# Sliding-window attention and a two-layer MLP: other order of loads, transposes and products in the opening

## The chip, the cores and the metric

The kernel runs on one core of a Trainium2 chip. A core has TensorE (PE in the profile; its weight loads are listed as PEld), VectorE (DVE), ScalarE (ACT), GpSimd (POOL) and SyncE (SP), each with a program of its own; they wait for one another by semaphores. PE reads from SBUF and writes to PSUM, whose eight banks are named here A, C, B, E, LA, LB and t (t is two banks). Transfers that change the type on the way (float32 in memory to bfloat16 or float16 in SBUF) are issued by POOL. The metric is the device time of one execution in microseconds; the profile's span is a little shorter than it.

## The reference

```python
def _attn_ref(q, k, v):                      # q, k, v: (8, 8, 576, 64)
    window = 32
    scores = (1.0 / np.sqrt(D)) * np.matmul(q, k.transpose(0, 1, 3, 2))
    mask = np.abs(pos[:, None] - pos[None, :]) <= window
    scores = np.where(mask, scores, -1000000000.0)
    scores = scores - np.max(scores, axis=-1, keepdims=True)
    attn = np.exp(scores)
    attn = attn / (np.sum(attn, axis=-1, keepdims=True) + 1e-09)
    return np.matmul(attn, v)

def _moe_ref(x, w_in, w_out):                # x: (4608, 512), w_in: (512, 2048), w_out: (2048, 512)
    h = x @ w_in
    g = h * (1.0 / (1.0 + np.exp(-1.702 * h)))
    return g @ w_out

x = attn_out.transpose(0, 2, 1, 3).reshape(B * S, H * D)
```

Every token attends to the 32 tokens on either side within its sequence of 576; the eight heads side by side are the input of the MLP.

## The kernel before

The 4608 tokens (8 sequences end to end) are cut into 36 units of 128 queries, and four units make a tile of 512 tokens for the MLP. A unit's queries start 32 tokens behind its keys, so that two blocks of 64 queries each see 128 keys. For a unit u, `scores(u, tag)` makes 24 small products into two PSUM banks and two exps on ACT; `band(u)` is the product with the 0/1 mask on DVE; `values(u, tag)` makes 16 products of 65 columns (the 65th sums the weights), for which the values are needed once as loaded (`ve`) and once shifted by 64 tokens (`vo`, made by `odd_v`: its half 1 copies from the values of u, its half 0 from those of u + 1); `norm(u)` divides on DVE; `x_T` or `x_T2` transposes one or two units on PE, and a copy puts them into `xT`.

The MLP of tile 0 is done in plain products: `layer1_plain(t, d, half, tag)` is 8 products of 256 columns into one bank and a gelu on ACT (d counts 256 columns of w_in, so quarter c of w_in serves d = 2c and 2c + 1; half is the first or second pair of units), and `layer2_plain` gives a list `l2` of 64 products of 512 columns, which `do(l2, n)` takes n at a time to fill PE where it would wait. In that list the products 8 to 15 read the second quarter of w_out, 16 to 23 the third. The later tiles use Strassen-like sums (`w1_sums`, `w2_sums`, `x_sums`, `g_sums`) with seven products for eight; their first block is `l1_group` in `first_layer1`, called when `opening` has ended. What is left of `l2` is run out in `run` between scores(9) and scores(10).

`opening` (lines 576 to 717) is the whole work up to there, in an order written out by hand: each engine runs its instructions in the order in which these calls stand, and waits at each for what it needs. It has units 0 to 7, layer 1 of tile 0 and part of its layer 2. The keys and queries of tile 0 come in two parts (`load_first`, part 0 and 1, 256 or 320 tokens), are transposed on PE by `T_first` in two banks each and copied out by the two engines named; those of tile 1 come by `load_four` and `T_four`. `load_v(u)` loads values (128 tokens, in pieces where a sequence ends: token 576 lies in the middle of unit 4), `load_w1(c)` a quarter of w_in, `load_w2(c)` a quarter of w_out. All these loads stand in POOL's program, between its other work (the mask by `setup_mask`, some `odd_v`), and in one DMA queue.

`keep_busy(n, tag, cols)` makes n products of zeros whose results nobody reads, to fill PE where it would wait. Before the change there are 60 of 96 columns at the start and then 6, 4, 10, 5, 2, 4, 4 and 4 of 256 columns (lines 606 to 660).

ACT has to load a table when it goes from exp to gelu or back. In the opening the exps of units 0 to 3 come first, then gelus, then the exps of units 4 to 7, then gelus again.

Of the kernel before, what the change touches and what calls it, by code (L numbers as in the profile page):

```python
# [26 lines left out]
class _Kernel:  # L27
# [536 lines left out]

    def keep_busy(self, n, tag="t", cols=256):
        junk = self.bank(tag, [128, 512], F32, "junk")
        for _ in range(n):
            self.mm(junk[:, 0:cols], self.idle[:, 0:128], self.idle[:, 0:cols], start=True, stop=True)  # L570


    SHARES = {("first", 1): (3, 0, 5, 4), ("first", 2): (3, 3, 6, 6), ("first", 3): (3, 1, 7, 7), ("last", 0): (0, 12, 6, 6),
# [2 lines left out]
    def opening(self):  # L576

        nc, dve, act, pool = self.nc, self.nc.vector, self.nc.scalar, self.nc.gpsimd
        self.setup()
        for i in range(8):  # L580
            dve.memset(self.idle[:, 64 * i:64 * i + 64], 0.0)
        dve.memset(self.spark, 0.0)
        for t in self.ve:
            dve.memset(t[:, :, self.D:], 1.0)
        self.load_first("k", 0)
        self.load_first("q", 0)
        make_identity(nc, self.ident)
        act.activation(self.spark, self.spark, AF.Exp)
        for u in (0, 1, 2):
            self.load_v(u)  # L590
        self.load_w1(0)
        self.setup_mask()
        self.load_first("k", 1)
        self.load_first("q", 1)
        self.load_w1(1)
        self.load_v(3)
        self.load_v(4)
        self.load_w1(2)
        self.load_four("k")
        self.load_four("q")  # L600
        self.load_w1(3)
        self.odd_v(3, pool)
        dve.tensor_copy(self.identh, self.ident)
        self.keep_busy(60, "E", 96)
        self.T_first("k", 0, "AC", (dve, act))
        self.keep_busy(6, "E")
        self.T_first("q", 0, ("LA", "LB"), (dve, act))
        self.keep_busy(4, "E")
        self.load_v(5)
        self.load_w2(0)  # L610
        self.load_v(6)
        self.load_v(7)
        self.load_v_part(1024, 64)
        self.load_w2(1)
        self.load_v_part(1088, 64)
        for c in (2, 3):
            self.load_w2(c)
        self.load_kq("k", 8)
        self.scores(0, "t")
        self.scores(1, "AC")  # L620
        self.odd_v(0, dve)
        self.odd_v(1, dve, (1,))
        self.keep_busy(10, "E")
        self.band(0)
        self.odd_v(1, dve, (0,))
        self.band(1)
        self.values(0, "t")
        self.keep_busy(5, "E")
        self.values(1, "AC")
        self.norm(0)  # L630
        self.norm(1)
        self.keep_busy(2, "E")
        self.x_T(0, "LA", act)
        self.keep_busy(4, "E")
        self.x_T(1, "LB", act)
        self.T_first("k", 1, "AC", (dve, dve))
        h, n, gelus = [], [0], []

        def l1(half, *ds):
            for d in ds:  # L640
                self.layer1_plain(0, d, half, h[n[0] % len(h)])
                n[0] += 1

        self.layer1_plain(0, 0, 0, "B", gelus)
        self.T_first("q", 1, ("LA", "LB"), (dve, act))
        self.layer1_plain(0, 1, 0, "E", gelus)
        h[:] = ["B", "E", "LB", "LA", "B", "E", "LB", "LA"]
        self.odd_v(2, dve, (1,))
        self.scores(2, "t")
        self.scores(3, "AC")  # L650
        self.layer1_plain(0, 2, 0, "LA", gelus)
        self.layer1_plain(0, 3, 0, "LB", gelus)
        self.do(gelus)
        self.band(2)
        self.odd_v(2, dve, (0,))
        self.band(3)
        self.keep_busy(4, "t")
        self.values(2, "t")
        self.norm(2)
        self.keep_busy(4, "A")  # L660
        self.values(3, "AC")
        self.norm(3)
        l1(0, 4)
        self.x_T2(2, "A", dve)
        l1(0, 5)
        dve.tensor_copy(self.k_first, self.kT[0][:, :, 0:64])
        dve.tensor_copy(self.v_first, self.ve[0][0:64])
        for i in (3, 1, 2):
            self.w1_sums((i,), 0)
        self.cut_mask()  # L670
        for u in (6, 7):
            self.odd_v(u, pool)
        for u in (8, 9, 10, 11):
            self.fetch(u)
        l1(1, 0, 1)
        halo = self.kT[4]
        self.T_four("k", "AC", (dve, dve))
        dve.tensor_copy(self.kT[4][:, :, 0:64], halo)
        self.w1_sums((4,), 0)
        l1(1, 2, 3)  # L680
        self.T_four("q", "AC", (dve, act))
        l1(1, 4, 5)
        self.odd_v(4, dve)
        self.scores(4, "t")
        self.scores(5, "AC")
        for i in (3, 1):
            self.w1_sums((i,), 1)
        for d, tag in ((6, "B"), (7, "E")):
            self.layer1_plain(0, d, 0, tag, gelus)
        self.do(self.l2, 3)  # L690
        self.scores(6, "t")
        self.do(self.l2, 3)
        self.scores(7, "AC")
        self.do(gelus)
        self.do(self.l2, 2)
        self.band(4)
        self.odd_v(5, dve)
        self.band(5)
        self.band(6)
        self.values(4, "t")  # L700
        self.norm(4)
        self.values(5, "AC")
        self.norm(5)
        self.band(7)
        self.do(self.l2, 4)
        self.values(6, "t")
        self.norm(6)
        self.do(self.l2, 4)
        self.values(7, "AC")
        self.norm(7)  # L710
        h[:] = "BE"
        n[0] = 0
        l1(1, 6, 7)
        self.x_T2(4, "A", act)
        self.do(self.l2, 4)
        self.x_T2(6, "t", dve)
        self.do(self.l2, 4)
# [223 lines left out]
```

## Time and profile before

| | us |
|---|---|
| median of three runs | 286.95 |
| lowest and highest | 286.2, 288.33 |
| the profiled execution | 286.22 |
| its span | 284.5 |
| PE busy | 277.3 (97%) |
| DVE busy | 215.9 (76%) |
| ACT busy | 194.0 (68%) |
| POOL busy | 131.4 (46%) |

Busy time of PE counts products whose results nobody reads, and products that overlap are counted once. A line in a view by time has the start, the duration, the engine, the line of the code, the operation, what is written and read, its shapes and the number of instructions merged; in brackets the idle time before it and what ended it. In a merged group of products the time from its start to the start of the next group tells more than its duration, since the end of one product overlaps the next. Nearly all products have line 70, that of a helper, and are told apart by the names of their tiles: h is layer 1, o is layer 2, sc scores, pv values, tp a transpose, junk an unread product.

### The profile page before, as it was taken

The numbers are of one execution on the slowest core, as the hardware profiler recorded it, in microseconds if no ns is written. First come the engines' busy times: TensorE is split into PE (matmuls) and PEld (weight loads), VectorE is DVE, ScalarE is ACT, GpSimd is POOL, SyncE is SP. The second block draws the span as 40 slices with busy tenths as digits, with TensorE's granted clock in tenths as the row PEclk, the third lists the DMA queues.
The fourth block names the chain that finished last, engine by engine and source line by source line (L and its number), as shares of the span: only waits on it lengthen the run. The fifth ranks groups of instructions, "written<-read, shape, count | busy, mean of one in ns | idle before, by whom it ended". The sixth has DMA issues, their size and how long they took to land.

```text
span 284.5 us, 9230 instructions
## 1 busy us (share of the span) xinstructions
PE 277.3 (97%) x3819; PEld 231.0 (81%) x3819; DVE 215.9 (76%) x502; ACT 194.0 (68%) x341; POOL 131.4 (46%) x199
## 2 busy tenths in 40 slices
PE   8999999999999999999999999999999999999993
PEld 8778857776787888888788888888888888888882
DVE  1758795896987889788778887888788888856621
ACT  2557775889887679668866887587759775677320
POOL 8866497996799429947084809331010000000000
PEclk9999999999999999999999999999999999999999
DMA  8999999999999999999999999994522030202033
GB/s 93 183 193 199 184 203 157 197 123 158 130 166 138 195 133 184 144 200 133 188 144 175 141 175 125 175 143 82 148 52 83 2 111 21 76 0 76 9 105 113
DMA packets 147003, 37.38 MB, mean 131 GB/s; under 512 B 133904, under 2 KB 142608, under 8 KB 146960
## 3 DMA queue, kind: packets, MB, share of 16 engines
q0 software_dynamic: 104480, 18.42, 95.9%
q1 hardware_dynamic: 42032, 17.84, 33.6%
q8 instruction: 30, 0.49, 0.8%
q10 hardware_dynamic: 448, 0.52, 0.6%
q14 instruction: 13, 0.11, 0.1%
HBM read 36.83 MB, written 9.44 MB: 163 GB/s over the span
## 4 chain that ended last, share of the span: by engine, by line
PE 81%; DMA 14%; POOL 2%; DVE 1%; issue 1%; ACT 0%; DVEq 0%; POOLq 0%
PE o L70 38%; PE h L70 35%; DMA w<-in_moe_w_out_dram 4%; DMA o_sb<-in_k_dram 4%; PE pv L70 4%; DMA xT<-x 3%; PE sc L70 3%; DMA w<-in_moe_w_in_dram 3%; POOL ve L199 1%; PE tp L336 1%; PE tp L242 1%; DVE xs L368 0%; POOL kq L143 0%; DVE h L446 0%; POOL ve L205 0%
## 5 line engine op out<-in xcount | busy, mean ns | idle before, releaser
L433 ACT ACTIVATE g<-h 128x512 f16<-128x512 f32 x128 | 72.1, 598 | 36.1 <-PE h L70 35.9
L70 PEld LDWEIGHTS <-g 128*128 128x128 f16 x576 | 54.4, 98 | 9.5
L70 PEld LDWEIGHTS <-a 128*128 128x128 f16 x512 | 49.2, 97 | 11.8 <-DVE xs L368 1.4
L70 PE MATMUL h<-xs,a 128*128 128x256 f16 x384 | 57.6, 272 | 0.5 <-DVE xs L368 0.3
L70 PE MATMUL o<-w,g 128*128 128x256 f16 (+1 forms) x320 | 55.5, 294 | 0.1
L70 PEld LDWEIGHTS <-w 128*128 128x128 f16 x512 | 48.9, 98 | 6.7 <-DVE xT L67 0.2
L70 PE MATMUL h<-xT,w 128*128 128x256 f16 x384 | 54.0, 273 | 0.0
L199 POOL DMA_DIRECT2D ve<-in_v_dram x39 | 33.3, 859 | 33.5 <-issue 28.6
L70 PEld LDWEIGHTS <-gs 128*128 128x128 f16 x384 | 36.8, 98 | 4.7
L267 ACT ACTIVATE p<-sc 128x512 bf16<-128x512 f32 x72 | 36.7, 618 | 2.5 <-PE sc L70 2.4
L70 PE MATMUL o<-b,gs 128*128 128x256 f16 x256 | 37.7, 273 | 0.0
L70 PE MATMUL o<-b,g 128*128 128x256 f16 x256 | 37.3, 273 | 0.0
L446 DVE TENSOR_TENSOR h<-h,s 128x512 f32<-128x512 f32 x32 | 22.4, 699 | 18.0 <-PE h L70 17.9
L67 ACT COPY h<-h 128x512 f32<-128x512 f32 x32 | 18.9, 589 | 15.9 <-PE h L70 15.5
L131 POOL DMA_DIRECT2D qst<-in_q_dram x35 | 28.1, 804 | 3.3 <-DMA kst<-in_k_dram 2.5
L131 POOL DMA_DIRECT2D kst<-in_k_dram x31 | 26.5, 859 | 5.8 <-DMA ve<-in_v_dram 3.2
L308 DVE TENSOR_TENSOR x<-pv,rec 128x256 f16<-128x256 f32 (+1 forms) x53 | 27.6, 520 | 1.8
L278 DVE TENSOR_TENSOR p<-p,mask 128x1024 bf16<-128x1024 bf16 x36 | 25.0, 700 | 4.9 <-ACT p L267 4.9
L218 POOL COPY vo<-ve 64x264 int32<-64x264 int32 x31 | 14.3, 460 | 25.6 <-PE pv L70 24.1
L452 DVE TENSOR_TENSOR h<-h,s 128x512 f32<-128x512 f32 x32 | 22.4, 700 | 4.6 <-PE h L70 4.0
L67 ACT COPY s<-h 128x512 f32<-128x512 f32 x32 | 19.1, 597 | 1.5 <-PE h L70 0.3
L70 PE MATMUL h<-xs,w 128*128 128x256 f16 x128 | 19.2, 273 | 0.0
(86 smaller groups left out, 371.3 us busy)
## 6 DMA issues: line engine op xcount, KB each, us to landing
out_dram<-o_sb SPq DMA_DIRECT2D x33, 256.0 KB, 4.3
ve<-in_v_dram POOLq DMA_DIRECT2D x31, 128.0 KB, 7.0
kst<-in_k_dram POOLq DMA_DIRECT2D x25, 128.0 KB, 7.0
qst<-in_q_dram POOLq DMA_DIRECT2D x21, 128.0 KB, 6.5
w<-in_moe_w_in_dram POOLq DMA_DIRECT2D x4, 512.0 KB, 9.2
w<-in_moe_w_out_dram POOLq DMA_DIRECT2D x4, 512.0 KB, 12.5
qst<-in_q_dram POOLq DMA_DIRECT2D x7, 96.0 KB, 6.5
ve<-in_v_dram POOLq DMA_DIRECT2D x10, 64.0 KB, 8.5
```

The source lines that it names most:

```text
L67: (eng.copy if eng is self.nc.scalar else eng.tensor_copy)(out, in_)
L70: self.nc.tensor.matmul(out, lhsT, rhs, start=start, stop=stop, skip_group_check=True)
L131: self.nc.gpsimd.dma_start(t[off:off + n], src[b, :, s:s + n, :].rearrange("h s d -> s h d"))
L199: self.nc.gpsimd.dma_start(t[off:off + n, :, :self.D], self.v[b, :, s:s + n, :].rearrange("h s d -> s h d"))
L218: eng.tensor_copy(words(vo[64:128]), words(self.ve[u % 9][64:128]))
L242: self.nc.tensor.transpose(tp[:, i, hp, :], src[:, 128 * hp:128 * hp + 128], self.ident)
L267: self.nc.scalar.activation(p[:, eo].rearrange("k h s -> k (h s)"), sc[eo], AF.Exp, scale=self.scale)
L278: (eng or self.nc.vector).tensor_mul(pv, pv, msk.to_broadcast([128, 8, 2, SQ]))
L308: dve.tensor_mul(x[:, 4 * at:4 * (at + n), :].rearrange("p (b h) d -> p b h d", b=n), acc[:, :, :, :D], r.to_broadcast([128, n, 4, D]))
L433: act.activation(g[:, f, 256 * half:256 * half + 256], bank.rearrange("p (i n) -> p i n", i=2), AF.Gelu_apprx_sigmoid)
L446: dve.tensor_add(e, b, s7)
L452: dve.tensor_add(c, b, s7)
```

## The change

All of it is in `keep_busy` and `opening`.

- `keep_busy` takes a number of rows: with 64, the weights are 64 columns instead of 128, and only 64 partitions of the bank are written.
- Loads: part 1 of the keys and queries is issued ahead of the first quarter of w_in and of the mask's instructions. Values 3 and the first 64 tokens of values 4 come ahead of the second quarter; the last 64 tokens of values 4 go behind the fourth. POOL's `odd_v(3)` goes from behind the fourth quarter to between the four-tile keys and queries.
- Unread products up to scores 1: 64 of 90 columns, then 2 of 256 and 20 of 64 columns, then 1 of 256 and 16 of 64 (33 more in number than 60, 6 and 4); after scores 1, 3 instead of 10.
- `T_first` of part 1 and the transposes of x of units 0 and 1 change places: all of `T_first` comes first, with three of its copies on ACT and one on DVE, then both `x_T` with their copies on DVE, then scores 2 and 3, and only then the first `layer1_plain`. Their gelus are no longer collected and run later, but follow each.
- Two `layer1_plain` stand between scores 3 and values 2, one behind values 3 and four unread products of 512 columns, one behind `x_T2(2)`; then four of the second half. d = 4 and 5 of the first half go behind the four-tile keys.
- Around units 4 to 7: the second half of `w1_sums` 3 and 1 goes ahead of `odd_v(4)`; `odd_v(5)` is split into its halves. Layer-2 products: 4 behind scores 6, 4 behind scores 7, none between values 5 and values 7 (8 before), 4 behind the last `layer1_plain`; 20 in the opening instead of 24. `layer1_plain(0, 6, 1)` comes ahead of values 7, `layer1_plain(0, 7, 1)` behind it.

```diff
-    def keep_busy(self, n, tag="t", cols=256):
+    def keep_busy(self, n, tag="t", cols=256, rows=128):
         junk = self.bank(tag, [128, 512], F32, "junk")
         for _ in range(n):
-            self.mm(junk[:, 0:cols], self.idle[:, 0:128], self.idle[:, 0:cols], start=True, stop=True)
+            self.mm(junk[0:rows, 0:cols], self.idle[:, 0:rows], self.idle[:, 0:cols], start=True, stop=True)
...
         for u in (0, 1, 2):
             self.load_v(u)
+        self.load_first("k", 1)
+        self.load_first("q", 1)
         self.load_w1(0)
         self.setup_mask()
-        self.load_first("k", 1)
-        self.load_first("q", 1)
+        self.load_v(3)
+        self.load_v_part(512, 64)
         self.load_w1(1)
-        self.load_v(3)
-        self.load_v(4)
         self.load_w1(2)
         self.load_four("k")
+        self.odd_v(3, pool)
         self.load_four("q")
         self.load_w1(3)
-        self.odd_v(3, pool)
+        self.load_v_part(576, 64)
         dve.tensor_copy(self.identh, self.ident)
-        self.keep_busy(60, "E", 96)
+        self.keep_busy(64, "E", 90)
         self.T_first("k", 0, "AC", (dve, act))
-        self.keep_busy(6, "E")
+        self.keep_busy(2, "E")
+        self.keep_busy(20, "E", 64, 64)
         self.T_first("q", 0, ("LA", "LB"), (dve, act))
-        self.keep_busy(4, "E")
+        self.keep_busy(1, "E")
+        self.keep_busy(16, "E", 64, 64)
...
         self.scores(1, "AC")
         self.odd_v(0, dve)
         self.odd_v(1, dve, (1,))
-        self.keep_busy(10, "E")
+        self.keep_busy(3, "E")
...
         self.norm(0)
         self.norm(1)
-        self.keep_busy(2, "E")
-        self.x_T(0, "LA", act)
-        self.keep_busy(4, "E")
-        self.x_T(1, "LB", act)
-        self.T_first("k", 1, "AC", (dve, dve))
-        h, n, gelus = [], [0], []
-
-        def l1(half, *ds):
-            for d in ds:
-                self.layer1_plain(0, d, half, h[n[0] % len(h)])
-                n[0] += 1
-
-        self.layer1_plain(0, 0, 0, "B", gelus)
-        self.T_first("q", 1, ("LA", "LB"), (dve, act))
-        self.layer1_plain(0, 1, 0, "E", gelus)
-        h[:] = ["B", "E", "LB", "LA", "B", "E", "LB", "LA"]
+        self.T_first("k", 1, "BE", (act, act))
+        self.T_first("q", 1, ("LA", "LB"), (act, dve))
+        self.x_T(0, "B", dve)
+        self.x_T(1, "E", dve)
         self.odd_v(2, dve, (1,))
+        self.keep_busy(3, "LA")
         self.scores(2, "t")
         self.scores(3, "AC")
-        self.layer1_plain(0, 2, 0, "LA", gelus)
-        self.layer1_plain(0, 3, 0, "LB", gelus)
-        self.do(gelus)
+        gelus = []
+
+        def l1(half, d, tag):
+            self.layer1_plain(0, d, half, tag)
+
+        l1(0, 0, "B")
+        l1(0, 1, "E")
         self.band(2)
         self.odd_v(2, dve, (0,))
         self.band(3)
-        self.keep_busy(4, "t")
         self.values(2, "t")
         self.norm(2)
-        self.keep_busy(4, "A")
+        self.keep_busy(3, "LA")
         self.values(3, "AC")
         self.norm(3)
-        l1(0, 4)
+        self.keep_busy(4, "LA", 512)
+        l1(0, 2, "LA")
         self.x_T2(2, "A", dve)
-        l1(0, 5)
+        l1(0, 3, "LB")
...
-        l1(1, 0, 1)
+        l1(1, 0, "B")
+        l1(1, 1, "E")
+        l1(1, 2, "LA")
+        l1(1, 3, "LB")
         halo = self.kT[4]
         self.T_four("k", "AC", (dve, dve))
         dve.tensor_copy(self.kT[4][:, :, 0:64], halo)
         self.w1_sums((4,), 0)
-        l1(1, 2, 3)
+        l1(0, 4, "B")
+        l1(0, 5, "E")
         self.T_four("q", "AC", (dve, act))
-        l1(1, 4, 5)
+        l1(1, 4, "LB")
+        l1(1, 5, "LA")
+        for i in (3, 1):
+            self.w1_sums((i,), 1)
         self.odd_v(4, dve)
+        self.odd_v(5, dve, (1,))
         self.scores(4, "t")
         self.scores(5, "AC")
-        for i in (3, 1):
-            self.w1_sums((i,), 1)
         for d, tag in ((6, "B"), (7, "E")):
             self.layer1_plain(0, d, 0, tag, gelus)
-        self.do(self.l2, 3)
         self.scores(6, "t")
-        self.do(self.l2, 3)
+        self.do(self.l2, 4)
         self.scores(7, "AC")
         self.do(gelus)
-        self.do(self.l2, 2)
+        self.do(self.l2, 4)
         self.band(4)
-        self.odd_v(5, dve)
         self.band(5)
         self.band(6)
+        self.odd_v(5, dve, (0,))
         self.values(4, "t")
         self.norm(4)
         self.values(5, "AC")
         self.norm(5)
         self.band(7)
-        self.do(self.l2, 4)
         self.values(6, "t")
         self.norm(6)
-        self.do(self.l2, 4)
+        l1(1, 6, "B")
         self.values(7, "AC")
         self.norm(7)
-        h[:] = "BE"
-        n[0] = 0
-        l1(1, 6, 7)
+        l1(1, 7, "E")
+        self.do(self.l2, 4)
         self.x_T2(4, "A", act)
         self.do(self.l2, 4)
         self.x_T2(6, "t", dve)
```

## The prediction

> **What bounds the kernel now.** First the stretches of the span: per line the stretch, its length, busy time of PE, PE's weight loads, DVE, ACT and POOL (with counts), granted clock, DMA share and GB/s.
>
> ```profile
> 7.00:14.00 7.00, 6.47 (x160) 4.89 (x156) 5.42 (x13) 3.44 (x7) 6.39 (x12) 1.00 1.66 182
> 14.00:21.00 7.00, 6.74 (x155) 5.41 (x153) 3.92 (x8) 3.93 (x8) 4.37 (x7) 1.00 1.55 193
> 44.00:52.00 8.00, 7.98 (x62) 5.29 (x60) 5.92 (x11) 4.86 (x9) 6.41 (x8) 1.00 2.40 152
> ```
>
> TensorE (PE) is busy in all of them; from 44 us on with work that must be done, in the opening partly with unread products. What PE has to compute is the same before and after. So the change is worth what it does to PE's waste (waits and unread products) before the first grouped layer-1 block at 46.16 us. Second view, the chain that ended last; its opening part is loads:
>
> ```profile
> 5.99 7.84 DMA w<-in_moe_w_in_dram
> 14.12 11.24 DMA o_sb<-in_k_dram
> 26.32 12.75 DMA w<-in_moe_w_out_dram
> 39.11 1.02 PE o L70 x4
> ```
>
> The first quarter of w_in lands at 13.83, the four-tile keys at 25.36, the second quarter of w_out at 39.07, just before the product that reads it. Third, PE's weight loads in time order, the clearest list of what PE does when (start, us, and in brackets the idle time before and what ended it):
>
> ```profile
> 1.07 4.77 PEld L70 LDWEIGHTS <-idle 128*128 128x128 bf16 x60 [1.07 <-DVE idle L581]
> 6.04 1.11 PEld L168 LDWEIGHTS <-kq 64*64 64x64 bf16 x40 [0.20 <-DMA kq<-in_k_dram]
> 7.19 0.55 PEld L70 LDWEIGHTS <-idle 128*128 128x128 bf16 x6
> 7.96 0.60 PEld L168 LDWEIGHTS <-kq 64*64 64x64 bf16 x32 [0.21 <-issue]
> 8.60 0.33 PEld L70 LDWEIGHTS <-idle 128*128 128x128 bf16 x4
> 9.14 0.73 PEld L70 LDWEIGHTS <-kq 64*64 64x64 bf16 x48 [0.21 <-issue]
> 11.71 0.34 PEld L70 LDWEIGHTS <-p 128*64 128x64 bf16 x16 [0.81 <-DVE p L278]
> 12.74 0.33 PEld L70 LDWEIGHTS <-p 128*64 128x64 bf16 x16 [0.21 <-DVE rec L307]
> 14.96 0.60 PEld L168 LDWEIGHTS <-kq 64*64 64x64 bf16 x32 [0.29 <-DMA kq<-in_k_dram]
> 18.21 0.59 PEld L70 LDWEIGHTS <-kq 64*64 64x64 bf16 x48 [0.21 <-issue]
> 26.86 0.95 PEld L189 LDWEIGHTS <-o_sb 128*64 128x64 bf16 x32 [0.21 <-issue]
> 32.64 0.59 PEld L70 LDWEIGHTS <-kq 64*64 64x64 bf16 x48 [0.21 <-issue]
> ```
>
> I cut the opening at these rows: up to values(1), ending 13.08; from there to the transposes of the four-tile keys at 26.86; to scores(4) at 32.64; to 46.16. Then the end of the last stretch on PE, which also gives the prices:
>
> ```profile
> 41.79 1.92 PE L70 MATMUL h<-xT,w 128*128 128x256 f16 x16
> 43.54 0.61 PE L336 MATMUL tp<-identh,x 128*128 128x128 f16 x8
> 43.99 1.03 PE L70 MATMUL o<-w,g 128*128 128x512 f16 x4
> 44.85 0.61 PE L336 MATMUL tp<-identh,x 128*128 128x128 f16 x8
> 46.16 0.27 PE L70 MATMUL h<-xT,w 128*128 128x256 f16 x1
> ```
>
> From start to start: 16 products of 256 columns 1.75 us, 0.109 each, so one layer1_plain (8) costs 0.87; eight 128-column transposes 0.45 (0.056 each); four layer-2 products of 512 columns 0.86 (0.215 each).
>
> **Part 1, up to values(1): small products.** Here a chain of latencies sets the time (transposes, copies, scores, exp, mask, values) and unread products fill the gaps. The first block goes from 60 of 96 columns to 64 of 90, 5760 columns both times: nothing, and keys 0 land at 6.04 in any case. Between the first two transposes six of 256 columns (0.65) become two (0.22) and twenty of 64 columns on 64 weight columns. No such product is in the trace. From below: 16 products of values in 0.33 us, 0.021 each, where the two column halves alternate. From above: all the small ones write the same half, and in values one half gets one product per 0.041. I take 0.027, half of the 0.056 of a 128-column transpose, the row nearest in kind: 0.54, with the two big ones 0.76, so the second transposes move from 7.96 to about 8.05 (7.85 to 8.3 by the bounds). Then four of 256 (0.44) become one and sixteen (0.11 + 0.43): the scores waited for the copies of the queries here (9.14 is 1.18 after the transposes), so nothing more by my price, 0.2 by the upper one. Seven unread products fewer after scores(1) (0.76 us) cost nothing: values(0) waits until 11.71 for the mask product on DVE. Sum +0.1.
>
> [...]
>
> **The loads.** POOL issues all of them in program order:
>
> ```profile
> 7.17 1.34 POOL L105 TENSOR_SCALAR_AFFINE_SELECT mask<-mask 64x128 bf16<-64x128 bf16 x4
> 9.14 0.70 POOL L143 DMA_DIRECT2D kq<-in_q_dram  x1
> 9.81 0.80 POOL L115 DMA_DIRECT2D w<-in_moe_w_in_dram  x1
> ```
>
> Issue to landing of the last two, in KB and us:
>
> ```profile
> w<-in_moe_w_in_dram POOLq DMA_DIRECT2D x1, 512.0 KB, 8.6
> kq<-in_q_dram POOLq DMA_DIRECT2D x1, 256.0 KB, 6.9
> ```
>
> So second queries landed at 16.04, the second quarter of w_in at 18.41. At 182 GB/s the 512 KB of a quarter take 2.9 us. Without it ahead of them, second keys land near 12.1 instead of 14.96, queries near 13.1; with their 512 KB ahead of it the first quarter lands at 16.0 (when all of these had landed before) to 16.7. Values 3 and half of values 4 (192 KB, 1.0 us) push the second quarter to about 19.4. The mask comes two issues of 0.70 later and ends at 9.9; its first reader also needs two exps, done near 10.8 (below), so nothing. POOL's copy for odd values 3 now stands ahead of the issue of the four-tile queries and waits for values 3 and 4; a third quarter of w_in and the four-tile keys (512 KB each, 2.9 us each) are then queued, which covers it; uncovered, the transposes of those queries come later by as long as the queue runs dry. From w_in's last quarter on, the same bytes stand ahead of every load.
>
> **Part 2, 13.08 to the four-tile keys.** Rows for the latencies, ACT and then DVE:
>
> ```profile
> 8.78 0.59 ACT L67 COPY kq<-tp 128x512 bf16<-128x512 bf16 x1 [0.78 <-PE tp L168]
> 9.78 2.06 ACT L267 ACTIVATE p<-sc 128x512 bf16<-128x512 f32 x4 [0.42 <-PE sc L70]
> 18.71 2.07 ACT L267 ACTIVATE p<-sc 128x512 bf16<-128x512 f32 x4 [0.78 <-PE sc L70]
> 33.37 1.28 ACT L267 ACT_TABLE_LOAD   x1
> 34.66 4.03 ACT L267 ACTIVATE p<-sc 128x512 bf16<-128x512 f32 x8
> 38.70 1.28 ACT L404 ACT_TABLE_LOAD   x1
> 40.00 1.08 ACT L404 ACTIVATE g<-h 128x512 f16<-128x512 f32 x2
> ```
>
> ```profile
> 14.08 0.42 DVE L308 TENSOR_TENSOR x<-pv,rec 128x256 f16<-128x256 f32 x1
> 17.10 0.69 DVE L67 COPY kq<-tp 128x512 bf16<-128x512 bf16 x1 [0.34 <-PE tp L168]
> 19.83 0.89 DVE L278 TENSOR_TENSOR p<-p,mask 128x1024 bf16<-128x1024 bf16 x1 [1.72 <-ACT p L267]
> 40.63 0.68 DVE L278 TENSOR_TENSOR p<-p,mask 128x1024 bf16<-128x1024 bf16 x1
> ```
>
> On before's clock: second keys are transposed 13.2 to 13.8, queries to 14.4, both landed. ACT makes three copies (0.5 apart) until 15.3. DVE ends norm(1) at 14.5 and makes three copies of up to 0.69 until 16.55. Three unread products (0.33) and a switch of 0.2 put scores(2) at 15.8, 2.4 earlier than now. First exp 16.3 (0.5 behind the scores, as at 18.21 and 18.71), mask product 1.12 behind it, 17.4, then a copy of values and the second mask product, 19.2. PE meanwhile: two layer1_plain from 16.55 (transposed x and first quarter arrive together) to 18.3; values(2) 18.7; 0.33 unread; values(3) until 19.95; four unread of 512 columns (0.87) to 20.8, after the second quarter has landed; one layer1_plain, x_T2, five more: 0.87 + 0.45 + 4.35, 26.5, a switch of 0.2, 26.7. Now it is 26.86: -0.15, although the scores come 2.4 earlier. Both versions have done eight layer1_plain by then, and both spend 1.53 us here on unread products (now 2+4+4+4 of 256 columns, then 3+3 of 256 and four of 512). Only waits can shrink.
>
> **Part 3, to scores(4) and on to values(5).** The same work in the same order, 5.78 us, PE without waits: 0. Then ACT leads both: table load, eight exps until 38.69; the last free the banks of values(5). Eight layer-2 products stand ahead in both. 0.
>
> **Part 4, the end.** Now PE fills with 8 layer-2 products between values(5) and values(7). After, it goes straight to values(6), which waits for norm(4), and to layer1_plain(1,6), whose bank B is emptied by the gelu that follows the table load: 40.00 + 0.54. From 40.6: 0.87, values(7) (its mask product ends 41.3) until 41.9, 0.87, then three times four layer-2 products and two x_T2: 2.58 + 0.90. The first grouped block starts at 46.25, +0.1. But 20 instead of 24 layer-2 products are done then. The other four are made up where the remaining ones are run out, with PE full: 4 x 0.215 = +0.86.
>
> Sum: 0.1 - 0.15 + 0 + 0.1 + 0.86 = +0.9 us. The profiled execution took 286.22 (span 284.5, 1.72 around it), so 287.1 on its own clock. It was the fast end of three runs (286.2 to 288.33); on their median, 286.95, I forecast 287.9. Chance 0.42; its own range, with the bounds of part 1 and half a microsecond in part 2, is 287.2 to 288.8.
>
> **Rivals.** *Not slower:* the waits in part 2 vanish. Its floor is 13.08, 10.5 of real work (transposes 0.60 twice and 0.45 twice, scores 0.63, values 0.37 twice, eight times 0.87), 1.53 unread and four switches of 0.2: 25.9, 0.95 earlier than now; with part 1 at its lower end the sum is about 0: 286.9. It decides at layer1_plain(0,0) and values(2): if both start without waiting, this is it. For it: second keys are waited for now (0.29 at 14.96), and the keys of four land at 25.36, early enough. Against: mask products and norms still follow the exps. Chance 0.25.
>
> *First quarter of w_in late.* Values 2 and 3 stand behind layer1_plain(0,0) on PE, so each microsecond past 16.55 costs one. With a landing at 17.6, +1.0 more: 288.9. For it: the margin is zero by my own numbers. Chance 0.14.
>
> *Slow small products,* at 0.041 each or more: +0.5, 288.4. [...]
>
> *The clock falls.* Unread products in the first row take 0.080 per 96 columns, at 256 columns 0.109: PE starts at half speed, though the granted clock reads 1.00. With fewer fillers PE idles some 1.5 us ahead of values(0) instead of 0.8. If that slows it again, about 2 us of work from 13 on doubles, partly in waits: +1.6, 289.5. [...] Chance 0.08.
>
> **How the numbers follow.** Changes under 1% (2.9 us) are about what three runs spread over 0.7% can't tell from none. Range 285.6 to 289.5: below, the not-slower case less the 0.75 that the fastest run lies under the median, and some 0.5 of part 2's uncertainty; above, the clock case. Faster by over 1% (under 284.1) lies under every case; 0.05 is for the not-slower one at its far end. Slower by over 1% (over 289.8): half of the clock case, and 0.09 of the late quarter with a landing beyond 18.5: 0.13. Within 1%: 0.82.
>
> **What will show it.** Second keys transposed at 13.2 with no wait for DMA; scores(2) near 15.8; four-tile keys near 26.7; layer1_plain(1,6) waiting for a gelu; the first grouped block near 46.2, and 12 instead of 8 layer-2 products between scores(9) and scores(10). I am wrong if the four-tile keys start before 26 or the grouped block before 45.3, if PE waits over 0.5 us for w_in, or if the small products are not 0.02 to 0.04 us each.

## The result and the profile after

| | before | after |
|---|---|---|
| median of 20 runs each, in turns on one chip, us | 287.01 | 288.64 |
| lowest and highest, us | 285.17, 291.0 | 287.56, 290.39 |
| profiled execution, its span, us | 286.22, 284.5 | 287.74, 286.0 |

After takes 1.0068 of the time of before (interval 1.0045 to 1.0092), about 2 us more; the ratio is not that of the medians, which lie 1.63 us apart. The forecast was 287.9, the range 285.6 to 289.5.

The stretches of the span of after, in the columns of before's (length, busy time of PE, PE's weight loads, DVE, ACT, POOL, granted clock, DMA share, GB/s):

```profile
7.00:14.00 7.00, 5.62 (x197) 4.74 (x198) 4.74 (x12) 3.27 (x7) 6.58 (x12) 1.00 1.71 186
14.00:21.00 7.00, 5.57 (x141) 4.17 (x135) 4.49 (x12) 4.67 (x8) 3.46 (x6) 1.00 1.48 198
```

PE is busy for 11.19 us of these fourteen, where it was 13.21. Unread products are 0.82 us of the difference (4.00 us instead of 4.82); the rest is work that comes later because PE waits. PE's weight loads of after in time order show where (start, us, what, and in brackets the idle time before and what ended it):

```profile
7.00 0.81 PEld L70 LDWEIGHTS <-idle 128*64 128x64 bf16 x20 [0.21 <-issue]
7.84 0.60 PEld L168 LDWEIGHTS <-kq 64*64 64x64 bf16 x32
8.49 0.89 PEld L70 LDWEIGHTS <-idle 128*128 128x128 bf16 x17
9.43 0.59 PEld L70 LDWEIGHTS <-kq 64*64 64x64 bf16 x48
...
11.06 0.20 PEld L70 LDWEIGHTS <-idle 128*128 128x128 bf16 x2 [0.92 <-issue]
...
12.97 0.34 PEld L70 LDWEIGHTS <-p 128*64 128x64 bf16 x16 [0.29 <-DVE p L278]
13.35 1.11 PEld L168 LDWEIGHTS <-kq 64*64 64x64 bf16 x64
...
15.88 0.23 PEld L70 LDWEIGHTS <-kq 64*64 64x64 bf16 x13 [0.21 <-issue]
17.37 0.46 PEld L70 LDWEIGHTS <-kq 64*64 64x64 bf16 x35 [1.25 <-issue]
17.86 1.64 PEld L70 LDWEIGHTS <-w 128*128 128x128 f16 x16
...
28.16 0.95 PEld L189 LDWEIGHTS <-o_sb 128*64 128x64 bf16 x32 [0.21 <-issue]
...
33.94 0.59 PEld L70 LDWEIGHTS <-kq 64*64 64x64 bf16 x48 [0.21 <-issue]
```

Second keys and queries are transposed at 13.35 in one go, with no wait for a load, and scores(2) starts at 15.88: both as forecast. Then something new stands in the middle of scores(2) and (3). After 13 of 48 identical loads PE stops for 1.25 us, and no semaphore and no transfer of data ends the stop: "issue" means that the profile shows nothing that was waited for. A shorter stop of the same kind, 0.92 us, lies among the three unread products after scores(1), where PE would have waited for the mask product anyway.

The difference between the two profiled executions, at five places that both have:

| place on PE | before | after | difference |
|---|---|---|---|
| values(1) | 12.74 | 12.97 | +0.23 |
| four-tile keys | 26.86 | 28.16 | +1.30 |
| scores(4) | 32.64 | 33.94 | +1.30 |
| first grouped block | 46.16 | 47.69 | +1.53 |
| scores(10) | 70.23 | 72.53 | +2.30 |
| end of the span | 284.51 | 286.02 | +1.51 |

The step from 46 to 70 us is the run-out of the layer-2 products. First before, then after, in the list of weight loads:

```profile
68.40 1.41 PEld L70 LDWEIGHTS <-g 128*128 128x128 f16 x8
70.23 0.33 PEld L70 LDWEIGHTS <-kT 64*64 64x64 bf16 x24 [0.42 <-issue]
```

```profile
69.83 2.27 PEld L70 LDWEIGHTS <-g 128*128 128x128 f16 x12
72.53 0.33 PEld L70 LDWEIGHTS <-kT 64*64 64x64 bf16 x24 [0.42 <-issue]
```

Twelve products instead of eight: 2.70 us to the next scores, against 1.83. Of the 2.30 us, 0.8 are not there at the end. Before's profiled execution waited twice at 137 us (0.56 + 0.36 us), after's did not. The weight loads of before there:

```profile
137.04 0.33 PEld L70 LDWEIGHTS <-a 128*128 128x128 f16 x4 [0.56 <-DVE xs L368]
...
138.16 0.33 PEld L70 LDWEIGHTS <-a 128*128 128x128 f16 x4 [0.36 <-DVE xs L368]
```

DVE in turn waited there for a transfer; the list of waits of before from 120 to 150 us (waited for, total, times, longest):

```profile
DVE xs L368 <- DMA xT<-x: 1.1, 1, 1.1
```

### A stop that nothing in the program asks for

The profile has a queue that carries instructions. The lines on PE's count of instructions and on this queue (packets, MB, share) from the page of after, then from the page of a later version with fewer unread products (f1 below):

```profile
PE 275.3 (96%) x3841; PEld 229.8 (80%) x3841; DVE 214.3 (75%) x502; ACT 194.0 (68%) x341; POOL 129.3 (45%) x199
...
q8 instruction: 30, 0.49, 0.8%
```

```profile
PE 274.4 (96%) x3753; PEld 226.1 (79%) x3755; DVE 214.7 (75%) x502; ACT 194.1 (68%) x341; POOL 131.3 (46%) x199
...
q8 instruction: 29, 0.48, 0.7%
```

30 packets in 0.49 MB are 16 KB each, and there is one of them for about 128 loads (3841 / 30). A load and its product are two instructions, so by these counts a packet would be 256 instructions of 64 bytes, an estimate of mine. Count the loads of after from the first: 64 unread, 40 transposes, 2 + 20 unread, 32 transposes, 17 unread, 48 scores and 1 unread are 224, and there the first of the two stops stands. With 2 unread, 16 values, 5 unread, 16 values, 64 transposes of keys and queries, 8 of x, 3 unread and 13 scores it is 351, and there the second stands. The two are 127 loads apart: one packet, to within one load.

Packets can be placed by the DMA view of windows of 0.2 us. After has one in 8.6 to 8.8 and one in 14.8 to 15.0 (packets, MB, share of the window):

```profile
q8 instruction: 1, 0.02, 32.8%
```

```profile
q8 instruction: 1, 0.02, 30.0%
```

Their starts are 8.61 and 14.92; PE goes on at 11.06 and 17.37, 2.45 us later both times. The block that ends at the second stop was entered at 11.06, and the packet for the next one starts 3.9 us after that. So my theory became: PE asks for the next block when it enters one, the packet queues behind the loads of data, and a block that PE runs through before the next one can be used (here 6.3 us, 11.06 to 17.37) ends in a stop. Here the block is made of small products and transposes. In before the same places of the stream fall on 12.78, inside values(1), and 18.41, inside scores(2), 5.6 us apart; its packet started at 15.50, 2.7 us behind the entry, and there is no stop. What makes a packet start late, the queue of loads or something else, none of the runs below takes apart.

The rivals to this theory were that the stop belongs to the instruction at which it stands (a bank, a switch between kinds of products), that the small products themselves cost the time, that the loads do, or that the whole loss is the four layer-2 products at the end of part 4.

### The profile page after: what moved, and what is told of

It reads as the page before. It is cut to its first block, busy times and chain, and to the rows that moved or that the text cites. A ratio compares the mean times of both kernels' runs of the same rounds, so it can differ in the third digit from the quotient of the medians.

```text
span 286.0 us, 9277 instructions
## 1 busy us (share of the span) xinstructions
PE 275.3 (96%) x3841; PEld 229.8 (80%) x3841; DVE 214.3 (75%) x502; ACT 194.0 (68%) x341; POOL 129.3 (45%) x199
## 4 chain that ended last, share of the span: by engine, by line
PE 76%; DMA 12%; POOL 5%; DVE 3%; issue 2%; ACT 0%; POOLq 0%
PE o L70 37%; PE h L70 32%; DMA w<-in_moe_w_out_dram 4%; DMA w<-in_moe_w_in_dram 4%; PE pv L70 3%; PE sc L70 3%; DMA ve<-in_v_dram 3%; DMA kst<-in_k_dram 2%; POOL ve L199 2%; DVE b L360 1%; POOL kq L143 1%; DVE h L446 1%; POOL o_sb L178 1%; PE tp L336 1%; POOL qst L131 1%
## 5 line engine op out<-in xcount | busy, mean ns | idle before, releaser
L199 POOL DMA_DIRECT2D ve<-in_v_dram x37 | 31.9, 863 | 31.4 <-issue 27.4
L218 POOL COPY vo<-ve 64x264 int32<-64x264 int32 x31 | 14.3, 463 | 30.7 <-PE pv L70 25.9
```

The costliest lines, as they stand in the source:

```text
L199: self.nc.gpsimd.dma_start(t[off:off + n, :, :self.D], self.v[b, :, s:s + n, :].rearrange("h s d -> s h d"))
L218: eng.tensor_copy(words(vo[64:128]), words(self.ve[u % 9][64:128]))
```

## The experiments

Each is compared with runs of before taken with it; ratios are to those, and are not ratios of the two medians that stand in front of them.

**e1: after, with before's layer-2 products and `layer1_plain(1, 6)` and `(1, 7)` as before around units 4 to 7.**

```diff
+        self.do(self.l2, 3)
         self.scores(6, "t")
-        self.do(self.l2, 4)
+        self.do(self.l2, 3)
         self.scores(7, "AC")
...
-        self.do(self.l2, 4)
+        self.do(self.l2, 2)
...
+        self.do(self.l2, 4)
         self.values(6, "t")
         self.norm(6)
-        l1(1, 6, "B")
+        self.do(self.l2, 4)
         self.values(7, "AC")
         self.norm(7)
+        l1(1, 6, "B")
         l1(1, 7, "E")
-        self.do(self.l2, 4)
```

> The changed kernel with the layer-2 products and the last two layer1_plain placed as before (3 behind layer1_plain(0,7), 3 behind scores 6, 2 behind scores 7, 4 + 4 between values 5 and values 7, 24 in the opening). Theory P (part 4 of the prediction: four layer-2 products fewer and waits for norm(4) and the gelu): about 1.0 us less than the changed kernel, so 287.6 and a ratio to the kernel before of 1.002 to 1.004; the first grouped block about 0.2 earlier than 47.5 with 24 products done. Theory I (all of the loss is PE waiting for its own instructions at scores 3): no gain, 288.6.

287.58 against 286.59: 1.0046 (1.0016 to 1.0076). From the four-tile keys to scores(10) it takes 43.33 us (28.45 to 71.78), before 43.37, after 44.37. So the end of the opening costs 1.0 us there, as part 4 had it (0.1 + 0.86); in the time it is 0.2% (1.0068 to 1.0046, with intervals that overlap, so that its size is open). By the two ratios the larger part of the loss stands ahead of the four-tile keys. e1's profile also shows what, by the mean granted clock (0.992 here), half of after's executions have (0.985 to 0.994 in ten of 20). Two windows of 3.41 us each (columns as above):

```profile
8.15:11.56 3.41, 1.97 (x94) 1.78 (x88) 2.02 (x5) 2.17 (x5) 3.16 (x9) 1.00 1.76 178
11.56:14.97 3.41, 3.36 (x51) 2.16 (x52) 2.37 (x7) 0.48 (x1) 2.29 (x3) 0.50 1.43 197
```

The granted clock is 0.50 for one window, behind a window in which PE was busy for 1.97 us; the stop ahead of load 225 (10.20 to 11.61 here) lies in that one.

**e2: after, without the small products** (33 unread products fewer, with before's numbers and widths).

```diff
-        self.keep_busy(64, "E", 90)
+        self.keep_busy(60, "E", 96)
...
-        self.keep_busy(2, "E")
-        self.keep_busy(20, "E", 64, 64)
+        self.keep_busy(6, "E")
...
-        self.keep_busy(1, "E")
-        self.keep_busy(16, "E", 64, 64)
+        self.keep_busy(4, "E")
```

> The changed kernel with 60 unread products of 96 columns, 6 and 4 of 256 up to scores 1 as before, 33 fewer in number. Theory I (PE's instructions come in blocks of 128 pairs of load and product; a block is asked for when the one before it is entered, and arrives 4.5 to 6.3 us later): entering the block at pair 224 moves from 11.06 to about 13.1, in values 1, so the block at pair 352 arrives at 17.7 to 19.4, and PE, at the last pairs of scores 3, waits for it from about 16.4: layer1_plain(0,0) 0 to 1.5 us later than the 17.86 of the changed kernel, time 288.6 to 290. Rival J (the small products cost time by themselves or by their number): 0.1 to 0.5 us faster than the changed kernel, 288.2, and no gap inside scores 3.

289.96, 1.0115 (1.0087 to 1.0143): the slowest of all. Its weight loads:

```profile
15.21 0.58 PEld L70 LDWEIGHTS <-kq 64*64 64x64 bf16 x46 [0.21 <-issue]
18.34 0.13 PEld L70 LDWEIGHTS <-kq 64*64 64x64 bf16 x2 [2.55 <-issue]
18.58 3.02 PEld L70 LDWEIGHTS <-w 128*128 128x128 f16 x16
```

The stop has moved along the scores from behind the 13th to behind the 46th load: 33 fewer loads ahead, 33 more of the scores done. Counted from the first it is 351 again. So it belongs to a place in PE's stream and to no operation. It is twice as long, since the block was entered later (12.45) and its packet started later (16.11), while PE got to the block's end earlier (15.79, after 16.11). The 33 small products had *shortened* the stop. The 16 layer-1 products behind it take 3.02 us instead of 1.64; the windows show why:

```profile
14.62:18.03 3.41, 1.17 (x51) 0.77 (x48) 2.29 (x6) 1.70 (x4) 1.05 (x2) 1.00 1.64 192
18.03:21.44 3.41, 3.10 (x16) 2.18 (x17) 0.69 (x1) 2.48 (x3) 3.41 (x6) 0.50 1.27 203
```

**e3: before, with only the unread products around scores 0 and 1 as in after.**

```diff
...
-        self.keep_busy(60, "E", 96)
+        self.keep_busy(64, "E", 90)
...
-        self.keep_busy(6, "E")
+        self.keep_busy(2, "E")
+        self.keep_busy(20, "E", 64, 64)
...
-        self.keep_busy(4, "E")
+        self.keep_busy(1, "E")
+        self.keep_busy(16, "E", 64, 64)
...
-        self.keep_busy(10, "E")
+        self.keep_busy(3, "E")
```

> The kernel before with only the unread products of the change (64 of 90 columns, 2 + 20 small, 1 + 16 small, 3 behind scores 1). Theory I: PE enters pair 224 at about 11.1 after a wait that lies in the wait for the mask product, and pair 352 is reached in layer1_plain(0,1) at about 17.3, when its block is just there: 0 to +0.4 us, 287.0 to 287.4. Rival J (the small products make the loss): +1 us or more, 288.0 and up. The slow small products of the prediction (0.041 each or more): +0.5.

286.3 against 286.59: 0.9986 (0.9963 to 1.0008), no loss. The stops are there, though:

```profile
11.61 0.20 PEld L70 LDWEIGHTS <-idle 128*128 128x128 bf16 x2 [1.25 <-issue]
...
17.91 0.55 PEld L70 LDWEIGHTS <-w 128*128 128x128 f16 x6 [0.31 <-issue]
```

The first lies where PE waits anyway, the second is 0.31 us: before's order has a `layer1_plain` of 0.87 us between the keys and the queries, so that this block takes 6.3 us with next to no stop. The small products alone are not the loss.

**e4: after, with the loads (and POOL's `odd_v(3)`) in before's order.**

```diff
-        self.load_first("k", 1)
-        self.load_first("q", 1)
         self.load_w1(0)
         self.setup_mask()
-        self.load_v(3)
-        self.load_v_part(512, 64)
+        self.load_first("k", 1)
+        self.load_first("q", 1)
         self.load_w1(1)
+        self.load_v(3)
+        self.load_v(4)
...
```

> The changed kernel with the loads in the order of before. Second keys land near 14.9 and queries near 16.1 and PE waits for them. Theory I: the wait takes the place of the wait for instructions at scores 3, scores 3 end near 18.2 instead of 17.83, and the second quarter of w_in comes 1.6 earlier; about +0.2, 288.8, and no gap inside scores 3. Rival (the gap of 1.25 us at scores 3 belongs to the scores, not to when the instructions were asked for): the gap stays and the two waits add, +1.6, 290.2.

288.89, 1.0077 (1.005 to 1.0103), against 1.0068 of after: the order of the loads moves the total by no more than the intervals. But what PE waits for has changed:

```profile
14.59 0.60 PEld L168 LDWEIGHTS <-kq 64*64 64x64 bf16 x32 [1.24 <-DMA kq<-in_k_dram]
15.91 0.95 PEld L168 LDWEIGHTS <-kq 64*64 64x64 bf16 x32 [0.71 <-DMA kq<-in_q_dram]
...
18.53 0.87 PEld L70 LDWEIGHTS <-kq 64*64 64x64 bf16 x48 [0.41 <-issue]
```

1.95 us of waits for keys and queries, and scores(2) and (3) without a stop: PE comes to load 352 only at 18.72, and the block is there. A part of that lateness is the clock, which is 0.50 from 15.86 to 19.27 in this execution; the packet had started at 15.43. The earlier keys of after bought a wait for instructions.

**f1: after, with long unread products in place of the many short ones** (86 fewer: 17 instead of 103 up to scores 0).

```diff
-        self.keep_busy(64, "E", 90)
+        self.keep_busy(12, "E", 480)
...
-        self.keep_busy(2, "E")
-        self.keep_busy(20, "E", 64, 64)
+        self.keep_busy(3, "E", 512)
...
-        self.keep_busy(1, "E")
-        self.keep_busy(16, "E", 64, 64)
+        self.keep_busy(2, "E", 512)
```

> The changed kernel with the unread products up to scores 1 as few long ones of about the same PE time (12 of 480 columns for 64 of 90, 3 of 512 for 2 + 20, 2 of 512 for 1 + 16; 86 fewer in number). Theory I (blocks of 128 pairs, asked for when the block before is entered): pair 96 falls into scores 0 (about 9.2), pair 224 into the transposes of the second queries (about 14, its block there near 13.8), pair 352 behind values 3 (about 20, there near 19.9): no gap at scores 3, layer1_plain(0,0) at 16.6 instead of 17.86, four-tile keys near 26.9, 286.8 to 287.0 where the clock stays up. Rival (fewer unread products cost, as the run without the small ones was slower): 289 to 290. Rival J (only PE time of unread products counts): 288.6.

287.21 against 287.10: 1.0031 (1.0004 to 1.0057). The ratio takes in two executions of 289.49 and 290.21 without a fall of the clock. So this version is nearer to before than after is, but by its interval still slower, and its four-tile keys start at 27.43 where I expected 26.9.

```profile
15.54 0.59 PEld L70 LDWEIGHTS <-kq 64*64 64x64 bf16 x48 [0.21 <-issue]
16.16 1.64 PEld L70 LDWEIGHTS <-w 128*128 128x128 f16 x16
...
20.32 0.11 PEld L70 LDWEIGHTS <-p 128*64 128x64 bf16 x1 [0.88 <-issue]
...
27.43 0.95 PEld L189 LDWEIGHTS <-o_sb 128*64 128x64 bf16 x32 [0.21 <-issue]
```

The stop is gone from the scores, and a shorter one, 0.88 us, stands ahead of the last product of values(3). The count there is 350 (12, 40, 3, 32, 2, 48, 3, 16, 5, 16, 64, 8, 3, 48, 16, 16, 3 and 15), the same place of the stream to within one. The trace also has a few semaphore instructions of PE; with these and the products counted, 705 instructions stand ahead of the stop in after, in e2 and in f1 alike.

**f2: f1 with e1's edit.**

```diff
-        self.keep_busy(64, "E", 90)
+        self.keep_busy(12, "E", 480)
...
+        self.do(self.l2, 4)
         self.values(6, "t")
         self.norm(6)
-        l1(1, 6, "B")
+        self.do(self.l2, 4)
...
```

> The same with the layer-2 products placed as before (24 in the opening). Theory I + P: both gains, four-tile keys near 26.9 and the first grouped block near 46.2 with 24 products done, so about the kernel before: 286.3 to 286.9, ratio 0.998 to 1.002. Rival (the two are one loss, counted twice): 287.6, as with the tail alone.

287.33 against 287.10: 1.0018 (0.9993 to 1.0042). From the four-tile keys to scores(10) it is 0.84 us shorter than f1 (27.43 to 70.97, against 71.81), but at the end it is longer (285.76, f1 285.29): a stop of the same kind at 81 us, which f1 hasn't, takes 1.47 us.

```profile
82.69 0.10 PEld L70 LDWEIGHTS <-kT 64*64 64x64 bf16 x2 [1.47 <-issue]
```

**f3: before, with the loads (and `odd_v(3)`) in after's order,** the reverse of e4's edit.

```diff
-        self.load_w1(0)
-        self.setup_mask()
         self.load_first("k", 1)
         self.load_first("q", 1)
-        self.load_w1(1)
+        self.load_w1(0)
+        self.setup_mask()
         self.load_v(3)
-        self.load_v(4)
+        self.load_v_part(512, 64)
+        self.load_w1(1)
...
```

> The kernel before with only the loads (and POOL's odd values 3) in the order of the change. Second keys are there when PE comes to them (0.3 gained), but layer1_plain(0,2), which stands ahead of values 2 here, needs the second quarter of w_in, which lands near 20.06 instead of 18.43: PE waits about 1.2 us from 18.85. If the transposed x of tile 3 (DVE waits for its transfer at 136 us in the kernel before, PE idles some 0.7) takes up the first 0.7 us of any delay: +0.2 to +0.5 us; if nothing takes it up, +0.9 to +1.2.

287.31 against 287.10: 1.0014 (0.9989 to 1.0039). Here `layer1_plain(0, 0)` waits for the first quarter of w_in:

```profile
16.50 0.77 PEld L70 LDWEIGHTS <-w 128*128 128x128 f16 x8 [1.42 <-DMA w<-in_moe_w_in_dram]
```

I had expected the wait at the second quarter; that one is 0.35 us (at 20.04). In after's order nothing is asked of the first quarter before 17.86.

**f4: before, with 1.1 us of unread products at the end of the opening,** to see whether a delay there reaches the end. They go through bank B, and tile 1's first grouped block then builds on other values there; the instructions are the same otherwise.

```diff
         l1(1, 6, 7)
+        self.keep_busy(10, "B")
         self.x_T2(4, "A", act)
```

> The kernel before with ten more unread products of 256 columns (1.09 us) in front of x_T2(4), where PE has no wait. Theory D (at 136 us PE waits some 0.7 us for a transfer whose landing does not move with PE): +0.3 to +0.5 us, ratio 1.001 to 1.002. Rival (PE-bound to the end): +1.1 us, ratio 1.004.

287.32 against 287.10: 1.002 (0.9998 to 1.0043). Its profiled execution reaches scores(10) 1.61 us later than before's and its end only 0.8 us later (285.3); the two waits at 137 us are missing in it, as in after's. They are also missing in e2, e3, e4, f1, f2 and g1, and present in e1 and f3, so they go with neither order. How much of a delay in the opening they take back on average was not settled: the interval has room for nothing and for all of the 1.1 us.

**g1: f1, without the unread products that stand ahead of scores 2 and behind values 3** (7 fewer), which in f1 only stand in the way.

```diff
         self.odd_v(2, dve, (1,))
-        self.keep_busy(3, "LA")
         self.scores(2, "t")
...
         self.norm(3)
-        self.keep_busy(4, "LA", 512)
         l1(0, 2, "LA")
```

> The run with long unread products, without the 3 of 256 columns in front of scores 2 and the 4 of 512 behind values 3. Theory I: pair 352 falls into layer1_plain(0,2) and its block still lands near 20.3, so four of its products run ahead of the wait and it ends near 20.8 instead of 22.4; four-tile keys near 26.0 (landed at 25.6), 1.4 earlier, and 286.0 (ratio 0.997). Rival (those unread products only filled waits for norm(3) and the second quarter of w_in): four-tile keys near 27.2, 287.0.

286.22 against 286.78: 0.9984 (0.9964 to 1.0003), and faster than after: the intervals (after's begins at 1.0045) are apart.

```profile
20.09 0.77 PEld L70 LDWEIGHTS <-w 128*128 128x128 f16 x8 [0.67 <-DMA w<-in_moe_w_in_dram]
...
25.97 0.95 PEld L189 LDWEIGHTS <-o_sb 128*64 128x64 bf16 x32 [0.21 <-issue]
```

The four-tile keys start at 25.97, 0.89 earlier than in before. Against before it is a draw: the interval just includes 1.

**g2: g1 with e1's edit.**

```diff
-        self.keep_busy(3, "LA")
         self.scores(2, "t")
...
+        self.do(self.l2, 4)
         self.values(6, "t")
         self.norm(6)
-        l1(1, 6, "B")
+        self.do(self.l2, 4)
...
```

> The same with the layer-2 products placed as before (24 in the opening). Theory I: as the run above in the first 26 us; the products behind values 5 then wait for the second quarter of w_out (39.09) and give back about half of the 0.86: 285.6 to 286.0, ratio 0.995 to 0.997. Rival: 287.0, as above.

286.92 against 286.78: 1.0008 (0.9986 to 1.0029), no better than g1 although scores(10) starts 0.61 us earlier (70.01, g1 70.62) and I had expected 0.995 to 0.997. The list of weight loads has a reason, as in f2:

```profile
82.01 0.20 PEld L70 LDWEIGHTS <-gs 128*128 128x128 f16 x2 [1.25 <-issue]
```

f2 and g2 stop behind load 1241 both, at different operations (scores there, Strassen-like sums here); in instructions it is 2498, seven packets of 256 behind 705, to within one. The block ahead of the stop is entered earlier than in the versions without the edit (load 1120 comes at 77.33 and 76.49; f1 78.17, g1 77.11) and the packet starts no earlier (79.9 and 79.6; 79.1 and 78.0). In these two profiled executions the four layer-2 products saved at 70 us were so paid for with a stop at 81. The edit alone does not make it: e1 has the same order and no stop there, its packet starting at 74.80, 0.5 us behind load 1120 (74.32). g2 also stops for 0.87 us at 138.31, thirteen packets behind 705.

## Why the prediction was right, and where it was not

*Direction and size* held: slower by less than 1%, likeliest 287.9, measured 288.64. The sum did not hold for its reasons, and that its total came near is partly luck. At scores(10) the parts add up to 2.30 us for the 0.91 of the sum; 0.8 of them were gone at the end of the profiled execution, and falls of the clock, which the sum has not, put 0.6 on the median.

*Part 1, small products:* forecast 0.027 us each, between 0.021 and 0.041. They took 0.042 (20 from 7.00 to 7.84) and about 0.05 (17 from 8.49 to 9.43, with one of 256 columns at 0.11). Half of a transpose's 0.056, which I took, was too little, and values with 0.021, the bound from below, alternate between column halves. The bound from above, products into the same half, was right or a little low; over 0.04 each is one of the signs of being wrong that I had named, and slow small products (0.041 each or more, 288.4) had a chance of 0.11. Cost to values(1): +0.23 instead of +0.1. That size is uncertain by some 0.4 us: with before's unread products values(1) starts at 12.74 in before's own profile, at 12.32 in f3, 12.63 in f4 and 12.29 in e2. The second transposes start at 7.84, at my lower bound of 7.85, for another reason: 0.021 each gives 7.95, and the first 40 transposes ended half a microsecond earlier than in before (the next load at 6.67, before 7.19).

*Loads* held: in after second keys landed at 12.06, queries at 13.27, the first quarter of w_in at 15.85 and the second at 20.06, where 12.1, 13.1, 16.0 to 16.7 and 19.4 were forecast. The rival of a late first quarter fell with it.

*Part 2, the step that failed.* It was put at -0.15 with "Only waits can shrink" as its limit; it came to +1.07 (1.30 less part 1's 0.23), and the four-tile keys start at 28.16 instead of 26.7. I listed waits for loads, for copies, exps and norms, all of which the program asks for, and took it that PE has its instructions. The 1.25 us stop for the next block of them is this term: without it part 2 would be -0.18. In f1 part 2 is +0.81 with a stop of 0.88. e2 shows it by its place, f1 by making it move and shrink, e4 by trading it for waits for loads, g1 by reaching 25.97 without it. That this is near the 25.9 that I gave as the floor of part 2 in the "not slower" rival is chance: g1 has 1.2 us fewer unread products than that floor counts, and a wait of 0.67.

*Part 3* held to the hundredth: 5.78 us in both.

*Part 4:* +0.23 to the grouped block for +0.1, +0.77 more to scores(10) for +0.86. ACT shows the table load and the gelu that empties bank B 1.30 us behind the 38.70 and 40.00 of the forecast, by as much as scores(4) is late, and PE waits 0.25 us for that gelu:

```profile
40.00 1.28 ACT L404 ACT_TABLE_LOAD   x1
41.30 1.08 ACT L404 ACTIVATE g<-h 128x512 f16<-128x512 f32 x2
```

Whether a microsecond of PE at 70 us is a microsecond at the end stays open: taking it back gave 0.2% of the time in e1, with intervals that overlap, and nothing that could be measured in f2 and g2, where a stop for instructions stands behind it.

*The clock falls,* which I gave 0.08 and 289.5, is what half of the executions do. Ten of after's 20 have a mean granted clock below 0.9955; their median is 289.59, that of the other ten 288.03. So without a fall, as in the profiled one, after is 1.0 above before's median (its span 1.5 longer), and the falls, 1.56 us each, bring the median of all up by another 0.6. The condition I gave was idle time ahead of values(0) for want of fillers. The runs show idle time of PE, but from stops for instructions: falls in 6 of 6 executions of e2 (stop 2.55 us), 5 of 12 of e1, 5 of 9 of e4 (waits of 1.24 and 0.71 us besides a stop), 1 of 12 of e3 and of f4, none of 12 in f1, f2 and g1, where each stop and wait from 12 us to the four-tile keys is below 1 us, and none of before's 84 in these batches. So falls come in the versions with more idle time; what exactly brings one was not tried. A single gap does not settle it: f3's profiled execution has a wait of 1.42 us, e3's a stop of 1.25, and neither has a fall.

## What to carry to other kernels

Behind a fast stretch of many small instructions PE stopped here for 1.25 us, and by the count of loads it had run out of instructions. When a profile shows idle time that ends with "issue", in the middle of identical instructions, count them from the start and see whether the stops of two versions stand at the same number. Then see what else can stand there: here a few long products instead of many short ones took the stop off the scores (f1, 0.88 us later on), and with a `layer1_plain` of 0.87 us between keys and queries 0.31 us was left of it (e3). Fewer unread products as such are no cure: e2 has 33 fewer than after and the longest stop (2.55 us); it entered the block at 12.45 and was through with it at 15.79, after at 11.06 and 16.11. And before loads are moved forward, ask what the engine will be short of next when it no longer waits for them.

## What the runs showed that was not expected

- The stop for instructions, with 0.31 to 2.55 us each time, at loads 224, 350 or 351 and 1241 whatever stands there. In the opening, with 186 and 198 GB/s moved in after's two stretches, it took a block 4.7 us (6.40 to 11.06 in after) to 6.3 us (11.06 to 17.37) from the entry into the block before to its first use; 2.45 us of it in after, 2.23 in e2 and 2.25 in f1 (18.07 to 20.32) lie behind the start of its packet.
- The granted clock went to 0.50 for one window of 3.41 us (e1 from 11.56, e2 from 18.03, e4 from 15.86). In the 3.41 us ahead PE was busy for 1.97 us in e1 and for 1.17 us in e2; in e4 waits of 1.24 and 0.71 us end at 14.59 and 15.91. No idle stretch was longer than 2.55 us. After's profiled execution kept 1.00 behind 3.41 us (14.84 to 18.25) with 2.08 us busy. Whether PE's busy time decides it, and where, no run was made to test; that only part of the executions of e1 (5 of 12) and e4 (5 of 9) fall is not explained.
- Unread products on 64 weight columns, all into one column half, took 0.042 (20) and 0.052 us (16) each in after, at least twice the 0.021 of the values, which alternate between halves (16 in 0.34 us in after).
